# Six instead of four of eight hidden blocks through the three-pass second product, in a fused attention and expert kernel

## The chip, the cores and the metric

The kernel runs on one core of one Trainium2 chip. The metric is the device time of one execution in microseconds (us), as a median of several runs. Five engines matter: TensorE (PE in the profile, with its weight loads as PEld), VectorE (DVE), ScalarE (ACT), GpSimd (POOL) and the SyncE queue (SP), which issues the transfers.

## The reference

The first half is an attention without softmax. The queries, keys and values have 4 batches, 4 heads, 1088 positions and 32 columns. Each key and query row is projected by two 8 x 32 matrices, and the 64 products of the two results are its features. Sums over the positions give a 64 x 32 matrix and a 64-vector for each head, and every query divides one product by the other. The second half takes the result as 4352 tokens of 128 columns and sends every token through all four experts:

```python
def phi(x):
    a, b = einsum('rd,bhsd->bhsr', S1, x), einsum('rd,bhsd->bhsr', S2, x)
    return einsum('bhsi,bhsj->bhsij', a, b).reshape(*x.shape[:-1], r * r)
kv, z = einsum('bhsf,bhsd->bhfd', phi(k), v), sum(phi(k), axis=2)
x = (phi(q) @ kv) / (phi(q) @ z + 1e-6)        # then 4352 tokens x 128
p = domain_probs / (domain_probs.sum(-1) + 1e-9)
for e in range(4):                             # w1[e] 128 x 1024, w2[e] 1024 x 128
    out += p[:, e:e+1] * (maximum(x @ w1[e], 0) @ w2[e])
```

All is float32.

## The kernel before

The tokens are cut into 11 chunks: 128, 448, six of 512, 320, 256 and 128 tokens. A chunk is worked off in 16 steps, `steps[i] = (m, kq)`, four for each expert, and each step holds two blocks of 128 hidden rows (`j` is 0 and 1). An expert thus has eight blocks, `k = 2 * f + j`.

A product in plain float32 is two matmul instructions in the profile. In most chunks it is replaced by three passes in the faster type `F32R`: each operand is split into a high part and a rest, and three products of parts make up the whole. The first product (tokens by `w1`) uses three passes for all eight blocks (lines 969, 970 and 989), in chunks 2 to 9 and for experts 2 and 3 of chunk 1. Between the second and the third of these passes ScalarE scales the sum in place (line 971). The second product (hidden by `w2`) uses three passes for four of the eight blocks: those where `in_three(k)` holds, which are the even ones. For such a block ScalarE makes the high part `ha` (line 993), and VectorE makes the rest `hb` (line 994) and a third operand `hc`, which the profile names hd (line 995). For an odd block ScalarE makes the plain hidden block `hid` (line 1001), and the second product is a float32 matmul. All second products are issued on line 1050, into two accumulators, `o0` and `o1`. The first two passes of a three-pass block go into `o0`, its third pass and the float32 product into `o1`.

The order of the work is written out by hand. Each block is one half of a step. `first(i)` issues the first product of the two blocks; the third pass of a block, and what ScalarE and VectorE do after it, is issued by `third()` behind the first two passes of the next block. `work()` runs pieces of the attention for later chunks after each block, at a rate that is worked out from how many pieces are still needed. `second(i, j)` is due three half steps behind its `first`. When the last block of an expert is done, `close(i)` calls `gather`: ScalarE has copied `o0` to `ev` (line 1070), VectorE adds `o1` (line 1112), and GpSimd multiplies by the gate and adds to the total (lines 1116 to 1119). Then `gather` loads a gate for a later chunk into the buffer that came free (line 344).

The parts of the weights are made while chunk 1 and the first steps of chunk 2 run: `weight_parts` for `w1`, `second_weight_parts` for `w2` (a group named vab in the profile, lines 750 and 753). Before that, `start()` makes the first batch's keys and the first 128 tokens. It also fills `sx`, `by8` and `own8` (lines 856 to 864), which only the later batches use: GpSimd copies and sets them, and VectorE turns `by8` into `own8`. The plain chunks 0 and 10 use float32 weights. For chunk 10 the weights are loaded a second time by `load_last()`, in the middle of chunk 9.

Of the kernel before, what the change touches and what calls it, by code (L numbers as in the profile page):

```python
# [24 lines left out]
def kernel(  # L25
# [30 lines left out]
    R = 8  # L56
# [7 lines left out]
    CW = 512  # L64
    GE = 160
    LA = 2
    SK, KS = 2, 1
    NK = FB // SK
    UNITS = [[P, 448, 512], [512, 320, 256], [448, 512, P], [384, 320, 384]]

    CHUNKS = [P, 448, 512] + [512] * 5 + [320, 256, P]
# [55 lines left out]
        eng.dma_start(s_raw[R * i : R * i + R, :], src.bitcast(I32))  # L127

    w1_of, w2_of = {}, {}

    def load_w1(e):
# [1 line left out]
        nc.sync.dma_start(w1_of[e][:, :], w1[e])  # L135

    def load_w2(e, k, to=None):
        n, which = ((SK - KS) * NK, slice(KS, SK)) if k else (KS * NK, slice(0, KS))
        w2_of[e, k] = cpool.tile([P, n * DM], F32, tag=f"w2_{e}{k}", name="w2_sb")[:, :] if to is None else to
        for i, s in enumerate(range(SK)[which]):  # L140
            nc.sync.dma_start(
                w2_of[e, k][:, NK * DM * i : NK * DM * (i + 1)].rearrange("p (g d) -> p g d", d=DM),
                w2[e].rearrange("(g s p) d -> s p g d", s=SK, p=P)[s],
            )
# [6 lines left out]
    def in_three(b):  # L151
        return b % SK < KS

    def split_at(b):
        return (b % SK - (0 if in_three(b) else KS)) * NK + b // SK

    load_rows(k, 0, "kn")
    load_rows(q, 0, "qn", slice(0, P))
# [37 lines left out]
    kT = cpool.tile([P, P * NT], F32, name="kT")  # L196
    nc.gpsimd.memset(kT[:, S:], 0.0)
    vx = cpool.tile([P, NT, H, D + 1], F32, name="vx")
    nc.gpsimd.memset(vx[:, :, :, D : D + 1], 1.0)
# [35 lines left out]
            on_side(lambda s: out[half[s], :], lambda s: weights[:, half[s]], lambda s: moving, **flags)  # L235


    def word(name, t=I32):
        return cpool.tile([R2, 2 * D], t, name=f"s_{name}")
# [12 lines left out]
    s_e, s_f, s_m, s_x, s_n = (word(n) for n in ("e", "f", "m", "x", "n"))  # L252
# [36 lines left out]


    gates = dram.tile([B, E, GE * 32 // E], F32, name="gates")
    pn = cpool.tile([P, GE], F32, name="pn")
    pt = cpool.tile([P, GE], F32, name="pt")
    dhalf = cpool.tile([P, G, 2], F32, name="dhalf")
    dsum = cpool.tile([P, G], F32, name="dsum")

# [42 lines left out]

    def load_gates(m, experts):  # L340
        for e in experts:
            gate[m, e] = mpool.tile([P, CW], F32, tag="gate", bufs=4, name="gate")
            for b, c, n, at in parts(m):
                nc.sync.dma_start(gate[m, e][:, at : at + n], gates[b, e, c : c + n].partition_broadcast(P))

# [423 lines left out]

    def second_weight_parts(e):  # L770

        w = w2_of[e, 0]
        vab = cpool.tile([P, 2, KS * NK * DM], F32R, tag=f"w1_{e}", name="vab")
        a, b = vab[:, 0], vab[:, 1]
        split(a, w, 4096.0)
        join(b, w, 4096.0, a.bitcast(F32), ALU.subtract)
        yield
        split(a, w, 1.0)
        d = cpool.tile([P, KS * NK * DM], F32R, tag=f"w2_{e}0", name="vd")[:, :]
        join(d, b.bitcast(F32), 1.0, a.bitcast(F32), ALU.subtract)  # L780
        w2_parts[e] = a, b, d
        yield

    w_last = {}
# [24 lines left out]
    def start():  # L809
# [46 lines left out]
        for h in range(H):  # L856
            for to, step, at in ((16 * (h // 2) + h % 2, 2, 0), (32 + R * h, 1, R)):
                nc.gpsimd.tensor_copy(
                    _ap(sx, 32 * h, 32, to, [[HP, 2], [step, R]]), _ap(s_T, 0, 32, at, [[D, 2], [1, R]])
                )  # L860
        for h in range(2):
            nc.gpsimd.memset(_ap(by8, 0, P, 32 * h, [[16, 2], [1, 8]]), 1.0 - h)
            nc.gpsimd.memset(_ap(by8, 0, P, 32 * h + 8, [[16, 2], [1, 8]]), 0.0 + h)
        nc.vector.transpose(own8[:, :], by8[:, :])

        n1 = UNITS[b][1]
        qT = apool.tile([P, QW], F32, tag="y", name="qT2")
        turns = query_turns(b, n, n1, qT)
# [9 lines left out]
            pass  # L878
        key_blocks(b, kv)
        gate_sums()  # L880

    def front():
        for b in range(B):
# [35 lines left out]
    def first(i, work, between=None):  # L919
# [2 lines left out]
        n, (e, f) = CHUNKS[m], divmod(kq, NP)  # L922
        if plain(m):
            third()
            hd = hidden()
            hid[i] = [hd[:, n * j : n * j + n] for j in range(2)]
            if i in begun_hp:
                hp = begun_hp.pop(i)
                half_columns(i, hp, HP)
            elif i in made_hp:  # L930
                hp = made_hp.pop(i)
            else:
                hp = psum(ps_h, "h")
                for j in range(2):
                    both(
                        hp[:, n * j : n * j + n],
                        w1_of[e][:, P * (2 * f + j) : P * (2 * f + j + 1)],
                        (x_last if m else x_first)[:, :],
                        start=True,
                        stop=True,  # L940
                    )
            if m and kq % 2:
                nc.vector.tensor_scalar(
                    out=hd[:, 0 : 2 * n], in0=hp[:, 0 : 2 * n], scalar1=0.0, scalar2=None, op0=ALU.max
                )
# [19 lines left out]
        for j in range(2):  # L965
# [6 lines left out]
            third()  # L972
            hid[i].append(None)
            begun.append((i, j, k, g, wd[:, e, w], xd_))
            work()
            if between and j == 0:
                between(0)

    def hidden():
        return mpool.tile([P, CW], F32, tag="hid", bufs=5, name="hid")  # L980

    begun = []

    def third():

        while begun:
            i, j, k, g, w, x = begun.pop(0)
            n = g.shape[-1]
            nc.tensor.matmul(g, w, x, start=False, stop=True, skip_group_check=True)  # L989
            if in_three(k):  # L990
                ha, hb, hc = (mpool.tile([P, CW], F32R, tag=f"h{i}", bufs=3, name=f"h{i}")[:, 0:n] for i in "abd")
                high = ha.bitcast(F32)
                nc.scalar.activation(ha, g, ACTF.Relu, scale=NEAR)  # L993
                nc.vector.scalar_tensor_tensor(out=hb, in0=g, scalar=0.0, in1=high, op0=ALU.max, op1=ALU.subtract)  # L994
                nc.vector.scalar_tensor_tensor(  # L995
                    out=hc, in0=high, scalar=R12, in1=hb.bitcast(F32), op0=ALU.mult, op1=ALU.subtract
                )
                hid[i][j] = ha, hb, hc
            else:
                hid[i][j] = hidden()[:, 0:n]  # L1000
                nc.scalar.activation(hid[i][j], g, ACTF.Relu)  # L1001

    def second(i, j=None):
# [48 lines left out]

        if j == 0:
            for args in o1_next:
                into(1, *args)
            o1_next.clear()
            w = slice(DM * split_at(k), DM * (split_at(k) + 1))  # L1060
            (va, vb, vd), (ha, hb, hc) = w2_parts[e], hd[j]
            into(0, va[:, w], ha)
            if f == 0:
                o0_next.append((vb[:, w], hb))
            else:
                into(0, vb[:, w], hb, f == NP - 1)
            o1_next.append((vd[:, w], hc))
            if f == NP - 1:
                evs[m, e] = mpool.tile([P, CW], F32, tag="ev", bufs=1, name="ev")
                nc.scalar.activation(evs[m, e][:, 0:n], acc[m, e][0][:, 0:n], ACTF.Copy, scale=1.0 + R12)  # L1070
            return
        for args in o0_next:
            into(0, *args)
        o0_next.clear()
        x = second_weight(e, k), hd[j]
        if f == 0:
            o1_next.append(x)
        else:
            if f == NP - 1:
                for args in o1_next:  # L1080
                    into(1, *args)
                o1_next.clear()
            into(1, *x, f == NP - 1)

    o0_next, o1_next, begun_o, evs = [], [], [False, False], {}

    def turn_back(m, src):

# [14 lines left out]
    def gather(m, e):  # L1103
# [80 lines left out]
    for i in range(len(steps) + LA):  # L1184
        if i < len(steps):
# [71 lines left out]
```

## Time and profile before

| | us |
|---|---|
| median of 3 runs (481.13 to 483.31) | 481.29 |
| the profiled execution's own time | 479.09 |
| its span, first to last instruction | 477.3 |
| PE busy | 465.8 |
| PE weight loads busy | 334.6 |
| DVE busy | 317.0 |
| ACT busy | 324.5 |
| POOL busy | 93.1 |

The granted TensorE clock was 0.999 of full speed in the profiled execution. Matmuls are pipelined, so the time from the start of one to the start of the next says what it costs, and not its own length. The stages of the profile that the text names are: the start, up to about 17 us; chunk 0 and the float32 experts of chunk 1, up to 58; experts 2 and 3 of chunk 1 and the first expert of chunk 2, with the preparation of weights, 60 to 99; the rest of the 512-token chunks, 99 to 403; the chunk of 320 tokens, 403 to 434; the one of 256, 434 to 458; and chunk 10, to the end.

### The profile page before, as it was taken

How to read it: one execution, taken by the hardware profiler on the slowest of the kernel's cores; microseconds unless marked ns; L12 is line 12 of the kernel's file. 1: busy time of each engine (PE TensorE's matmuls, PEld its weight loads, DVE VectorE, ACT ScalarE, POOL GpSimd, SP SyncE). 2: the span in 40 equal slices, each digit the busy share in tenths (PEclk: the TensorE clock that was granted, in tenths of full speed). 3: DMA queues.
4: the chain of work that ended last, by engine and by line, in shares of the span. 5: the costliest groups of instructions: out<-in, count | busy, mean ns of one | idle time of the engine just before them, and what ended most of it. 6: DMA issues, size and time to landing. Idle time of an engine off the chain costs nothing.

```text
span 477.3 us, 8152 instructions
## 1 busy us (share of the span) xinstructions
PE 465.8 (98%) x2869; PEld 334.6 (70%) x2869; DVE 317.0 (66%) x586; ACT 324.5 (68%) x694; POOL 93.1 (20%) x122
## 2 busy tenths in 40 slices
PE   8899998989999999999999999999999999999997
PEld 6775566666667677666666676666666667888987
DVE  5836689857676579666586569566667576676542
ACT  4354587675777677676857777676777776788841
POOL 6210122200222122211022122212221112131120
PEclk9999999999999999999999999999999999999999
DMA  7808122441403212441413210042302300221800
GB/s 214 289 21 211 23 66 69 110 119 31 129 22 92 53 44 68 127 107 35 140 23 90 47 34 23 23 104 42 95 25 62 92 14 16 57 37 28 273 1 18
DMA packets 51232, 36.71 MB, mean 77 GB/s; under 512 B 26840, under 2 KB 45560, under 8 KB 51192
## 3 DMA queue, kind: packets, MB, share of 16 engines
q1 hardware_dynamic: 51176, 36.20, 28.9%
q8 instruction: 22, 0.36, 0.3%
q14 instruction: 18, 0.15, 0.1%
q10 hardware_dynamic: 16, 0.00, 0.0%
HBM read 31.11 MB, written 5.08 MB: 76 GB/s over the span
## 4 chain that ended last, share of the span: by engine, by line
PE 90%; DVE 4%; ACT 2%; DMA 1%; POOL 1%; issue 1%; SPq 0%; ACTq 0%; DVEq 0%; POOLq 0%
PE o L1050 38%; PE h L989 12%; PE h L970 11%; PE h L969 11%; PE h L230 4%; PE o L230 3%; PE n L230 3%; PE h L956 3%; PE o L1042 2%; PE f L679 1%; DMA qb<-qd 1%; DVE hb L994 1%; DVE hd L995 1%; PE f L414 1%; ACT h L971 1%
## 5 line engine op out<-in xcount | busy, mean ns | idle before, releaser
L971 ACT ACTIVATE h<-h 128x512 f32<-128x512 f32 (+3 forms) x272 | 147.9, 544 | 106.4 <-PE h L970 104.9
L994 DVE SCALAR_TENSOR_TENSOR hb<-h,ha 128x512 fp32r<-128x512 f32 (+3 forms) x136 | 85.6, 630 | 108.4 <-ACT ha L993 108.0
L969 PE MATMUL h<-xa,wa 128*128 128x512 f32 (+3 forms) x272 | 137.4, 505 | 0.0
L1050 PE MATMUL o<-hid,w_sb 128*128 128x512 f32 (+3 forms) x272 | 126.8, 548 | 0.0
L989 PE MATMUL h<-xd,wd 128*128 128x512 f32 (+3 forms) x272 | 106.0, 390 | 1.8 <-ACT h L971 1.6
L995 DVE SCALAR_TENSOR_TENSOR hd<-ha,hb 128x512 fp32r<-128x512 f32 (+3 forms) x136 | 96.7, 711 | 9.3
L970 PE MATMUL h<-xb,wb 128*128 128x512 f32 (+3 forms) x272 | 100.3, 369 | 0.0
L1118 POOL TENSOR_TENSOR ev<-ev,gate 128x512 f32<-128x512 f32 (+3 forms) x27 | 31.9, 1182 | 261.7 <-DVE ev L1112 250.3
L1001 ACT ACTIVATE hid<-h 128x512 f32<-128x512 f32 (+3 forms) x136 | 75.1, 552 | 0.2 <-PE h L989 0.2
L993 ACT ACTIVATE ha<-h 128x512 fp32r<-128x512 f32 (+3 forms) x136 | 74.6, 549 | 0.0
L969 PEld LDWEIGHTS h<-xa,wa 128*128 128x128 f32 x272 | 51.2, 188 | 26.6 <-issue 19.8
L970 PEld LDWEIGHTS h<-xb,wb 128*128 128x128 f32 x272 | 51.3, 188 | 25.9 <-issue 19.1
L989 PEld LDWEIGHTS h<-xd,wd 128*128 128x128 f32 x272 | 51.0, 187 | 22.6 <-ACT h L971 14.7
L1050 PE MATMUL o<-ha,vab 128*128 128x512 f32 (+3 forms) x136 | 62.6, 460 | 0.0
L1050 PEld LDWEIGHTS o<-hid,w_sb 128*128 128x128 f32 x272 | 48.6, 188 | 8.3 <-issue 0.2
L1050 PE MATMUL o<-hd,vd 128*128 128x512 f32 (+3 forms) x136 | 52.2, 384 | 2.1 <-DVE ev L1112 2.1
L1050 PE MATMUL o<-hb,vab 128*128 128x512 f32 (+3 forms) x136 | 52.5, 386 | 0.8 <-DVE hb L994 0.8
L1119 POOL TENSOR_TENSOR total<-total,ev 128x512 f32<-128x512 f32 (+3 forms) x27 | 37.8, 1399 | 2.1
L1050 PEld LDWEIGHTS o<-hb,vab 128*128 128x128 f32 x136 | 25.6, 189 | 11.0 <-issue 5.3
L1050 PEld LDWEIGHTS o<-ha,vab 128*128 128x128 f32 x136 | 25.6, 188 | 9.5 <-issue 6.1
L1050 PEld LDWEIGHTS o<-hd,vd 128*128 128x128 f32 x136 | 25.5, 188 | 7.3 <-DVE ev L1112 3.1
L1116 POOL TENSOR_TENSOR total<-ev,gate 128x512 f32<-128x512 f32 (+3 forms) x9 | 10.9, 1215 | 89.7 <-issue 31.0
(158 smaller groups left out, 436.5 us busy)
## 6 DMA issues: line engine op xcount, KB each, us to landing
gate<-gates SPq DMA_DIRECT2D x16, 256.0 KB
kn<-in_k_dram SPq DMA_DIRECT2D x4, 544.0 KB
vn<-in_v_dram SPq DMA_DIRECT2D x16, 128.0 KB
w_sb<-in_moe_w_dram SPq DMA_DIRECT2D x4, 512.0 KB
w_sb<-in_moe_w_dram SPq DMA_DIRECT2D x8, 256.0 KB
w_last<-in_moe_w_dram SPq DMA_DIRECT2D x4, 512.0 KB
gate<-gates SPq DMA_DIRECT2D x8, 224.0 KB
qn<-in_q_dram SPq DMA_DIRECT2D x2, 544.0 KB
```

The source lines that it names most:

```text
L230: nc.tensor.matmul(out(s), weights(s), moving(s), **flags)
L969: nc.tensor.matmul(g, wa[:, e, w], xa, start=True, stop=False)
L970: nc.tensor.matmul(g, wb[:, e, w], xb, start=False, stop=True)
L971: nc.scalar.activation(g, g, ACTF.Copy, scale=1.0 + R12)
L989: nc.tensor.matmul(g, w, x, start=False, stop=True, skip_group_check=True)
L993: nc.scalar.activation(ha, g, ACTF.Relu, scale=NEAR)
L994: nc.vector.scalar_tensor_tensor(out=hb, in0=g, scalar=0.0, in1=high, op0=ALU.max, op1=ALU.subtract)
L995: nc.vector.scalar_tensor_tensor(out=hc, in0=high, scalar=R12, in1=hb.bitcast(F32), op0=ALU.mult, op1=ALU.subtract)
L1001: nc.scalar.activation(hid[i][j], g, ACTF.Relu)
L1050: nc.tensor.matmul(acc[m, e][o][:, 0:n], w, h, start=not begun_o[o], stop=last)
L1118: nc.gpsimd.tensor_tensor(out=ev[:, 0:n], in0=ev[:, 0:n], in1=g, op=ALU.mult)
L1119: nc.gpsimd.tensor_tensor(out=total[m][:, 0:n], in0=total[m][:, 0:n], in1=ev[:, 0:n], op=ALU.add)
```

## The change

Six blocks of the eight, numbers 0, 1, 2, 4, 5 and 6, now take three passes in the second product, and 3 and 7 stay in float32. The weights of `w2` are loaded in runs of neighbouring blocks (two transfers for the six, two for the two, where there was one each). Their parts grow from 512 to 768 columns for each expert; the low part lies in two pieces, of 256 and 512 columns, so each VectorE operation on it becomes two. The third pass of a block is issued with the second product of the next block or a later one (`o1_next`). `third()` no longer issues the two VectorE operations; a new `lower()` does, after it and ahead of `work()`. In the one half step of an expert in which the previous expert is closed, the closing comes ahead of `lower()` and `work()`, where it came behind the pieces. The filling of `sx`, `by8` and `own8` moves from `start()` into `later_weights()`, called in step 8. To make room, some buffers share or shrink: `gate` from four to two (and the loads are issued two experts ahead), `hid` from five to four, `pn`, `pt`, the words of the start and the last expert's reloaded `w2` lie in tiles of others; `hd` gets four instead of three.

```diff
-    SK, KS = 2, 1
-    NK = FB // SK
+    THREE = (0, 1, 2, 4, 5, 6)
+    OTHER = [b for b in range(FB) if b not in THREE]
+    N3 = len(THREE)
...
     def load_w2(e, k, to=None):
...
+        for b, z in runs:
+            at = split_at(b)
             nc.sync.dma_start(
...
+                w2_of[e, k][:, DM * at : DM * (at + z - b)].rearrange("p (g d) -> p g d", d=DM),
+                w2[e, P * b : P * z].rearrange("(g p) d -> p g d", p=P),
+            )
+
+    def in_three(b):
+        return b in THREE
...
-            gate[m, e] = mpool.tile([P, CW], F32, tag="gate", bufs=4, name="gate")
+            gate[m, e] = mpool.tile([P, CW], F32, tag="gate", bufs=2, name="gate")
...
     def second_weight_parts(e):
-        w = w2_of[e, 0]
-        vab = cpool.tile([P, 2, KS * NK * DM], F32R, tag=f"w1_{e}", name="vab")
-        a, b = vab[:, 0], vab[:, 1]
+        w, n = w2_of[e, 0], N3 * DM
+        vab = cpool.tile([P, F], F32R, tag=f"w1_{e}", name="vab")
+        vb = cpool.tile([P, 2 * n - F], F32R, tag=f"vb_{e}", name="vb")
+        a, lows = vab[:, 0:n], [(0, F - n, vab[:, n:F]), (F - n, n, vb[:, :])]
         split(a, w, 4096.0)
-        join(b, w, 4096.0, a.bitcast(F32), ALU.subtract)
+        for c, z, b in lows:
+            join(b, w[:, c:z], 4096.0, a[:, c:z].bitcast(F32), ALU.subtract)
         yield
         split(a, w, 1.0)
-        d = cpool.tile([P, KS * NK * DM], F32R, tag=f"w2_{e}0", name="vd")[:, :]
-        join(d, b.bitcast(F32), 1.0, a.bitcast(F32), ALU.subtract)
+        d = cpool.tile([P, n], F32R, tag=f"w2_{e}0", name="vd")[:, :]
+        for c, z, b in lows:
+            join(d[:, c:z], b.bitcast(F32), 1.0, a[:, c:z].bitcast(F32), ALU.subtract)
...
             if e == 0:
-                w_last[0] = apool.tile([P, E, KS * NK * DM], F32, tag="kp", name="w2_last")
-            load_w2(e, 0, w_last[0][:, e])
+                w_last[0] = apool.tile([P, E - 1, N3 * DM], F32, tag="kp", name="w2_last")
+                w_last[1] = cpool.tile([P, N3 * DM], F32, tag="kT", name="w2_last")
+            load_w2(e, 0, w_last[0][:, e] if e < E - 1 else w_last[1][:, :])
...
+    def later_weights():
+        for h in range(H):
+            for to, step, at in ((16 * (h // 2) + h % 2, 2, 0), (32 + R * h, 1, R)):
+                nc.gpsimd.tensor_copy(
...
+        nc.vector.transpose(own8[:, :], by8[:, :])
...
-            work()
-            if between and j == 0:
+
+            if j == 0 and i >= 2 and steps[i - 2][1] % NP == NP - 1 and not plain(steps[i - 2][0]):
                 between(0)
+                lower()
+                work()
+            else:
+                lower()
+                work()
+                if j == 0:
+                    between(0)
...
+    def lower():
+        while to_lower:
+            g, high, hb, hc = to_lower.pop(0)
+            nc.vector.scalar_tensor_tensor(out=hb, in0=g, scalar=0.0, in1=high, op0=ALU.max, op1=ALU.subtract)
+            nc.vector.scalar_tensor_tensor(
+                out=hc, in0=high, scalar=R12, in1=hb.bitcast(F32), op0=ALU.mult, op1=ALU.subtract
+            )
...
+        x = hd[j]
+        if in_three(k):
+            if k > 1 and o1_next:
+                into(1, *o1_next.pop(0))
+            (va, vb, vd), (ha, hb, hc) = w2_parts[e][split_at(k)], x
+            into(0, va, ha)
+            into(0, vb, hb, k == THREE[-1])
+            o1_next.append((vd, hc))
+            if k == THREE[-1]:
                 evs[m, e] = mpool.tile([P, CW], F32, tag="ev", bufs=1, name="ev")
                 nc.scalar.activation(evs[m, e][:, 0:n], acc[m, e][0][:, 0:n], ACTF.Copy, scale=1.0 + R12)
         else:
+            while o1_next and (k == FB - 1 or len(o1_next) > 1):
+                into(1, *o1_next.pop(0))
+            into(1, second_weight(e, k), x, k == FB - 1)
...
-        if not plain(m + 1):
-            load_gates(m + 1, [e])
+        later = m + (e + 2) // E
+        if not plain(later):
+            load_gates(later, [(e + 2) % E])
...
+            elif i == 8:
+                later_weights()
             elif i == 5:
                 store_gates()
-                load_gates(1, range(E))
+                load_gates(1, range(2))
```

More of the change, by code (lines that the diff above doesn't have):

```diff
@@ L137, in load_w2, with split_at @@
     def load_w2(e, k, to=None):
-        n, which = ((SK - KS) * NK, slice(KS, SK)) if k else (KS * NK, slice(0, KS))
-        w2_of[e, k] = cpool.tile([P, n * DM], F32, tag=f"w2_{e}{k}", name="w2_sb")[:, :] if to is None else to
-        for i, s in enumerate(range(SK)[which]):
+        of = OTHER if k else THREE
+        w2_of[e, k] = cpool.tile([P, len(of) * DM], F32, tag=f"w2_{e}{k}", name="w2_sb")[:, :] if to is None else to
+        runs = []
+        for b in of:
+            if runs and b == runs[-1][1]:
+                runs[-1][1] += 1
+            else:
+                runs.append([b, b + 1])
+        for b, z in runs:
+            at = split_at(b)
             nc.sync.dma_start(
-                w2_of[e, k][:, NK * DM * i : NK * DM * (i + 1)].rearrange("p (g d) -> p g d", d=DM),
-                w2[e].rearrange("(g s p) d -> s p g d", s=SK, p=P)[s],
-            )
+                w2_of[e, k][:, DM * at : DM * (at + z - b)].rearrange("p (g d) -> p g d", d=DM),
+                w2[e, P * b : P * z].rearrange("(g p) d -> p g d", p=P),
+            )
+    def in_three(b):
+        return b in THREE
+    def split_at(b):
+        return (THREE if in_three(b) else OTHER).index(b)
     def second_weight(e, b):
@@ L149, in second_weight @@
         return w2_of[e, 0 if in_three(b) else 1][:, DM * at : DM * (at + 1)]
[L151 to L155, printed above, removed]
     load_rows(k, 0, "kn")
@@ L195 @@
     nc.gpsimd.memset(sx[:, :], 0.0)
-    kT = cpool.tile([P, P * NT], F32, name="kT")
+    kT = cpool.tile([P, P * NT], F32, tag="kT", name="kT")
     nc.gpsimd.memset(kT[:, S:], 0.0)
@@ L235, in both @@
             on_side(lambda s: out[half[s], :], lambda s: weights[:, half[s]], lambda s: moving, **flags)
-    def word(name, t=I32):
-        return cpool.tile([R2, 2 * D], t, name=f"s_{name}")
     def bits(out, in0, s1, op0, s2=None, op1=ALU.bypass):
@@ L251 @@
     shl, shr = ALU.logical_shift_left, ALU.logical_shift_right
-    s_e, s_f, s_m, s_x, s_n = (word(n) for n in ("e", "f", "m", "x", "n"))
+    words = apool.tile([R2, 5, 2 * D], I32, tag="y", name="words")
+    s_e, s_f, s_m, s_x, s_n = (words[:, i, :] for i in range(5))
     s_hl = cpool.tile([32, 2 * D], F32, name="s_hl")
@@ L291 @@
     gates = dram.tile([B, E, GE * 32 // E], F32, name="gates")
-    pn = cpool.tile([P, GE], F32, name="pn")
-    pt = cpool.tile([P, GE], F32, name="pt")
+    pn = mpool.tile([P, GE], F32, tag="ob", bufs=1, name="pn")
+    pt = mpool.tile([P, GE], F32, tag="total", bufs=1, name="pt")
     dhalf = cpool.tile([P, G, 2], F32, name="dhalf")
@@ L770, in second_weight_parts @@
     def second_weight_parts(e):
-        w = w2_of[e, 0]
-        vab = cpool.tile([P, 2, KS * NK * DM], F32R, tag=f"w1_{e}", name="vab")
-        a, b = vab[:, 0], vab[:, 1]
+        w, n = w2_of[e, 0], N3 * DM
+        vab = cpool.tile([P, F], F32R, tag=f"w1_{e}", name="vab")
+        vb = cpool.tile([P, 2 * n - F], F32R, tag=f"vb_{e}", name="vb")
+        a, lows = vab[:, 0:n], [(0, F - n, vab[:, n:F]), (F - n, n, vb[:, :])]
         split(a, w, 4096.0)
-        join(b, w, 4096.0, a.bitcast(F32), ALU.subtract)
+        for c, z, b in lows:
+            join(b, w[:, c:z], 4096.0, a[:, c:z].bitcast(F32), ALU.subtract)
         yield
         split(a, w, 1.0)
-        d = cpool.tile([P, KS * NK * DM], F32R, tag=f"w2_{e}0", name="vd")[:, :]
-        join(d, b.bitcast(F32), 1.0, a.bitcast(F32), ALU.subtract)
-        w2_parts[e] = a, b, d
+        d = cpool.tile([P, n], F32R, tag=f"w2_{e}0", name="vd")[:, :]
+        for c, z, b in lows:
+            join(d[:, c:z], b.bitcast(F32), 1.0, a[:, c:z].bitcast(F32), ALU.subtract)
+        w2_parts[e] = [
+            tuple(x[:, DM * i - c : DM * i - c + DM] for x, c in ((a, 0), next((x, c) for c, z, x in lows if DM * i < z), (d, 0)))
+            for i in range(N3)
+        ]
         yield
@@ L852, in start @@
             nc.gpsimd.tensor_copy(_ap(sq, 32 * h, 32, 32 * h, [[R2, 2], [1, R2]]), _ap(s_T, 0, 32, 0, [[D, 2], [1, R2]]))
[L856 to L864, printed above, removed]
         n1 = UNITS[b][1]
@@ L880, in start @@
         gate_sums()
+    def later_weights():
+        for h in range(H):
+            for to, step, at in ((16 * (h // 2) + h % 2, 2, 0), (32 + R * h, 1, R)):
+                nc.gpsimd.tensor_copy(
+                    _ap(sx, 32 * h, 32, to, [[HP, 2], [step, R]]), _ap(s_T, 0, 32, at, [[D, 2], [1, R]])
+                )
+        for h in range(2):
+            nc.gpsimd.memset(_ap(by8, 0, P, 32 * h, [[16, 2], [1, 8]]), 1.0 - h)
+            nc.gpsimd.memset(_ap(by8, 0, P, 32 * h + 8, [[16, 2], [1, 8]]), 0.0 + h)
+        nc.vector.transpose(own8[:, :], by8[:, :])
     def front():
@@ L974, in first @@
             begun.append((i, j, k, g, wd[:, e, w], xd_))
-            work()
-            if between and j == 0:
+            if j == 0 and i >= 2 and steps[i - 2][1] % NP == NP - 1 and not plain(steps[i - 2][0]):
                 between(0)
-    def hidden():
-        return mpool.tile([P, CW], F32, tag="hid", bufs=5, name="hid")
-    begun = []
+                lower()
+                work()
+            else:
+                lower()
+                work()
+                if j == 0:
+                    between(0)
+    def hidden():
+        return mpool.tile([P, CW], F32, tag="hid", bufs=4, name="hid")
+    begun, to_lower = [], []
+    def lower():
[5 more added lines that the diff above has]
+            )
     def third():
@@ L990, in third @@
             if in_three(k):
-                ha, hb, hc = (mpool.tile([P, CW], F32R, tag=f"h{i}", bufs=3, name=f"h{i}")[:, 0:n] for i in "abd")
+                ha, hb, hc = (
+                    mpool.tile([P, CW], F32R, tag=f"h{i}", bufs=4 if i == "d" else 3, name=f"h{i}")[:, 0:n] for i in "abd"
+                )
                 high = ha.bitcast(F32)
                 nc.scalar.activation(ha, g, ACTF.Relu, scale=NEAR)
[L994 to L997, printed above, removed]
+                to_lower.append((g, high, hb, hc))
                 hid[i][j] = ha, hb, hc
@@ L1051, in into @@
             begun_o[o] = True
[L1056 to L1068, printed above, removed]
+        x = hd[j]
[7 more added lines that the diff above has]
+            if k == THREE[-1]:
                 evs[m, e] = mpool.tile([P, CW], F32, tag="ev", bufs=1, name="ev")
                 nc.scalar.activation(evs[m, e][:, 0:n], acc[m, e][0][:, 0:n], ACTF.Copy, scale=1.0 + R12)
[L1071 to L1077, printed above, removed]
-        else:
[L1079 to L1085, printed above, removed]
+        else:
+            while o1_next and (k == FB - 1 or len(o1_next) > 1):
+                into(1, *o1_next.pop(0))
+            into(1, second_weight(e, k), x, k == FB - 1)
+    o1_next, begun_o, evs = [], [False, False], {}
     def turn_back(m, src):
```

## The prediction

> **What bounds the kernel now.** I read the page's busy row and its chain first.
>
> ```profile
> PE 465.8 (98%) x2869; PEld 334.6 (70%) x2869; DVE 317.0 (66%) x586; ACT 324.5 (68%) x694; POOL 93.1 (20%) x122
> PE 90%; DVE 4%; ACT 2%; DMA 1%; POOL 1%; issue 1%; SPq 0%; ACTq 0%; DVEq 0%; POOLq 0%
> ```
>
> PE carries the time, and no other engine is busy for more than 70% of the span. So a cheaper product pays, as long as the engine that pays for it keeps room. The timeline of PE in a 512-token chunk gives the two prices:
>
> ```profile
> 247.12 0.40 PE L1050 MATMUL o<-hd,vd 128*128 128x512 f32 x1
> 247.35 0.40 PE L1050 MATMUL o<-ha,vab 128*128 128x512 f32 x1
> 247.59 0.40 PE L1050 MATMUL o<-hb,vab 128*128 128x512 f32 x1
> 247.82 0.39 PE L969 MATMUL h<-xa,wa 128*128 128x512 f32 x1
> ...
> 248.75 1.02 PE L1050 MATMUL o<-hid,w_sb 128*128 128x512 f32 x2
> 249.21 0.79 PE L969 MATMUL h<-xa,wa 128*128 128x512 f32 x1
> 249.84 0.39 PE L970 MATMUL h<-xb,wb 128*128 128x512 f32 x1
> ```
>
> From start to start a fast pass takes 0.233 us (247.12 to 247.82 is three of them, 0.70). The float32 pair starts at 248.75, and the fast pass behind it is over when the next starts, at 249.84; less 0.23 for that pass, the pair takes 0.86.
>
> The groups by form give VectorE's price for a three-pass block, the windows its load by stage (PE, PEld, DVE, ACT, POOL in this order):
>
> ```profile
> L995 DVE SCALAR_TENSOR_TENSOR hd<-ha,hb 128x512 fp32r<-128x512 f32 x96 | 75.3, 784 | 6.6
> L994 DVE SCALAR_TENSOR_TENSOR hb<-h,ha 128x512 fp32r<-128x512 f32 x96 | 66.1, 688 | 83.7 <-ACT ha L993 83.5
> ```
>
> ```profile
> 60.00:99.00 39.00, 36.25 (x211) 25.86 (x210) 33.53 (x57) 29.65 (x64) 7.99 (x6) 1.00 0.31 78
> 99.00:403.00 304.00, 301.95 (x1441) 207.17 (x1440) 205.14 (x337) 218.17 (x424) 56.30 (x40) 1.00 0.25 65
> 403.00:434.00 31.00, 30.74 (x177) 26.84 (x176) 20.92 (x42) 24.88 (x69) 7.18 (x7) 1.00 0.19 40
> ```
>
> The same windows asked for lines 994 and 995 alone give 6.64 and 7.72 us, then 64.21 and 73.25, then 7.77 and 8.52. The average of 66% hides that DVE is at 86% from 60 to 99.
>
> The timeline of the start shows a chain of another kind:
>
> ```profile
> 11.22 1.43 POOL L858 COPY sx<-s_T 32x16 f32<-32x16 f32 x8
> 12.99 0.24 DVE L864 STREAM_TRANSPOSE own<-by 128x64 f32<-128x64 f32 x1 [1.65 <-POOL pn L299]
> 13.59 0.49 DVE L459 TENSOR_TENSOR kvz<-f,own 128x128 f32<-128x128 f32 x2
> 13.94 0.44 PE L230 MATMUL n<-qp,kvz 128*64 128x128 f32 x4 [1.93 <-DVE kvz L459]
> ```
>
> DVE stands 1.65 us for GpSimd to fill sx and by8, and PE stands 1.93 for DVE.
>
> **The change part by part.**
>
> *The start.* Without lines 856 to 864 in front of it, DVE goes on at 11.34 instead of 13.16. Then kvz waits only for its sums, whose matmuls end at about 11.8, so PE starts at about 12.2 and not at 13.94: **-1.7 us**. The moved work does not vanish: GpSimd is idle from about 20.4 until it copies ring at 26.57, so its 1.9 us in step 8 have cover, and own8 costs DVE 0.24 us behind a GpSimd that has then finished. Without that cover it would be the old 1.65 us on DVE. Bounds: 0 (if the first weights, issued at 5.85, land late) and -1.9.
>
> *PE's saving.* A block moved to three passes saves 0.86 - 0.70 = 0.16 us at 512 columns. Stage 99 to 403 has 94 rows of line 994, 23.5 experts of four; two blocks more each make 47 x 0.16 = **-7.5 us**. The TensorE page of the Trainium skill (TensorE: Matmul & The Clock Gate, Back-to-back issue gap) gives 2.5 ns on top of the streaming, 216 ns for 512 columns. By that estimate a block would save 0.21 us and the stage 10.0; the trace's 0.233 decides.
>
> *VectorE in 99 to 403.* Lines 994 and 995 grow by half: 205.14 + 137.46/2 = 273.9 us, of 304 - 7.5 = 296.5, or 92%. It fits on average, so I looked expert by expert in DVE's timeline, from the first ha pass of one expert to that of the next, and added the gaps over 0.12 us. Two more blocks need about 3.0 us (1.5 each, from a line 994's start to the end of its share), and the expert gets 0.32 shorter. Five stretches have less room: those from 130.8 (2.14 idle), 182.9 (3.14), 236.0 (2.72), 289.1 (3.27) and 354.8 (2.57), in which pieces of the attention pile up. With each one's own price for the two blocks they are short by 1.15, 0.19, 0.62, 0.10 and 1.01, together **+3.1 us**, which I take as stalls of PE. The bounds are 0, as a hb of an undisturbed block is ready 2.5 us before its pass (end 248.90, used at 251.44) and can soak up a short excess, and 10.6, which the slow rival prices.
>
> *VectorE in 60 to 99.* Here 33.53 us are used of 39. Half of 14.36 adds 7.2. The parts of w2 add: their two VectorE operations of 512 columns become two of 256 and two of 512, so two more of 0.425 (line 994 at 256 columns) for each expert, and three of the four experts fall here: 2.5. The sum is 43.3, 4.3 over the stage. About 1.0 can be carried as lag into the next stage, which has room: **+3.3 us**, and PE's own saving there (four blocks at 0.13, two at 0.16) is lost. ScalarE's splits grow too, by about 0.22 us each (0.591 less 0.374, line 971 at 512 and 256 columns), six of them here, against 9 idle us: nothing, or 1.3 if they lie on the path. Bounds: +1 (two and a half us carried, some idle filled) and +6 (none carried, DVE idle 1.5 us as now at 68.6).
>
> *Closing first.* PE and its loads wait six times for DVE's add of o1, 2.1 and 3.1 us together, overlapping. With the add ahead of the pieces I take **-0.5**, between 0 and -2.1. But the add itself waits for PE's last product, and the new expert's hb of block 1, which did not exist before, is queued behind it, with hc and the pieces behind that; PE's second product of block 1 waits for this hb.
>
> *320 and 256 columns.* At 320 the DVE sum is 20.92 + 8.15 = 29.1 us, of 31 less PE's saving of 0.9 (8 blocks at 0.11), 97%: **-0.2**, between -0.9 and +1. At 256, line 971's mean is 0.374, the two Relu forms 0.38, and the copy of o0 0.39: 8 x 0.757 + 0.39 = 6.45 us of ScalarE for an expert, whose period is 6.53. ScalarE decides and gets nothing less: 0, between -0.7 and +0.5.
>
> *Third passes a block later, buffers, transfers.* The later pass gives hc 1.4 us more; buffers add no wait where their reader is three half steps behind, which four hid tiles still cover. SP issues eight more transfers of w2 in the start (0.49 us each, its queue free from 18.5 until the gates at 22.68) and four more in the last load (0.44 each, issued from 441.8, used from 458): 0. If the first batch of gates slipped by the 3.9 us, batch 1 would too; it lands at about 42 and its turn comes at 61.7.
>
> *Sum.* -1.7 - 7.5 + 3.1 + 3.3 - 0.5 - 0.2 = -3.5. The profiled execution took 479.09 (span 477.3), so it would take 475.6. The median of the runs is 2.2 above that execution; on it the same sum gives 481.3 - 3.5 = **477.8**.
>
> The Trainium skill speaks against the change in one place (Perfetto Trace Analysis, Identifying the Most-Contended Engine): TensorE is to be judged by its weight loads, VectorE by its occupancy. By that, VectorE at about 85% becomes the most contended engine, ahead of the loads' 70%, and the -7.5 would be worth nothing, so the sum would be +4. The rows show PE without idle time at 70% of loads, so I follow the spacing of the passes.
>
> **The rivals.** *Slower: the closing's queue on DVE.* From the end of an expert's last product, hb of block 1 is ready after the add and itself, some 1.46 us; PE asks for it after the first product of a block, two passes, another first product and one pass, 2.1 us. That leaves 0.64, and the next hb has as little. The attention's other DVE work is (205.14 - 137.46 - 15.37)/188 = 0.28 us a block, but comes in lumps of 0.7 to 0.96. If each closing costs 0.45 us, stage 99 to 403 loses 10.6 instead of 3.1; with all 4.3 in 60 to 99 and +0.5 at 320: -1.7 - 7.5 + 10.6 + 4.3 + 0.5 = +6.2, **487.5**. The kernel as a whole gets slower from 0.19 us a closing on. For it: DVE's 92%. Against it: PE passed DVE's backlog of 238 to 243 without a wait for hb.
>
> *No change: the saving is given back.* The closings cost 0.25, 5.9 us, in place of 3.1, the rest as forecast: -0.7, **480.6**.
>
> *Faster still: the lag covers everything.* No stall in 99 to 403, +1.5 in 60 to 99, -0.9 at 320: -1.7 - 7.5 + 1.5 - 0.5 - 0.9 = -9.1, **472.2**.
>
> **How the numbers follow.** Forecast 0.36, faster still 0.14, no change 0.24, slower 0.26. A measurement of this kernel tells apart about 0.5%, 2.4 us. The forecast and the faster case lie below 478.9, so faster is 0.50, same 0.24, slower 0.26. The forecast's own range is 474 to 479. The range 472 to 486.5 leaves out half of the faster case and some of the slower, under 2 in 10.
>
> **What would show it.** Right: line 1050 with 136 rows of hid fewer and 68 more of each pass; PE's kvz wait gone; DVE near 400 us; PE idle mostly between 60 and 99; an expert at 512 columns in 12.1 us where it took 12.4. Wrong: PE waiting for hb (line of `lower`) at most closings; ScalarE behind DVE so that line 971 comes late; a stage from 60 to 99 that is no longer than now.

## The result, and the profile after

The changed kernel takes 508.31 us (median of 4 runs, 507.68 to 509.14), the kernel before 481.21 us beside it (4 runs, 479.55 to 483.31). The ratio is 1.057, with an interval of 1.054 to 1.061: slower by 27 us, where 3.5 less was forecast. The profiled execution took 507.68, its span is 505.9.

The page of the changed kernel, its busy row and the engines' shares of the chain that ended last:

```profile
PE 465.4 (92%) x2937; PEld 350.0 (69%) x2937; DVE 404.9 (80%) x730; ACT 330.6 (65%) x694; POOL 93.5 (18%) x122
PE 59%; DVE 26%; ACT 6%; issue 5%; DMA 3%; POOL 0%; DVEq 0%; SPq 0%; ACTq 0%
```

VectorE's 404.9 us are what the forecast expected ("near 400"), and 80% is far from full. Yet the chain, which was 90% PE and 4% DVE, is now 59% and 26%. VectorE has room on average and still holds PE up. What PE waits for, in the view of waits (engine, what it issues and line, what it waits for: us in total, times, longest):

```profile
PE o L1082 <- DVE hb L1012: 13.8, 16, 2.3
PE f L685 <- DVE qT L539: 11.8, 7, 2.3
PE f L420 <- DVE kT L377: 5.4, 3, 3.1
PE f L420 <- DVE fs L430: 2.5, 2, 2.1
```

These are 33.5 us. In the kernel before, PE's waits for VectorE came to 5.4 in all (`ev` 2.1, `kvz` 1.9, `hb` 0.8, `kT` 0.6). Only the first row is the wait that the prediction named; the other three are the attention's own passes on PE, whose operands (the transposed rows qT and kT, the features fs) stand in the same queue of VectorE.

The two operations of a three-pass block by form, and the windows (PE, PEld, DVE, ACT, POOL, granted clock, share and rate of the DMA):

```profile
L1013 DVE SCALAR_TENSOR_TENSOR hd<-ha,hb 128x512 fp32r<-128x512 f32 x144 | 116.0, 806 | 8.3
L1012 DVE SCALAR_TENSOR_TENSOR hb<-h,ha 128x512 fp32r<-128x512 f32 x144 | 98.4, 683 | 47.0 <-ACT ha L1028 46.3
```

```profile
60.00:99.00 39.00, 30.03 (x186) 23.06 (x187) 36.36 (x64) 25.36 (x52) 7.32 (x6) 0.96 0.31 74
99.00:403.00 304.00, 279.77 (x1380) 204.09 (x1379) 249.54 (x402) 204.55 (x390) 51.10 (x36) 0.98 0.25 61
403.00:434.00 31.00, 30.18 (x147) 22.32 (x146) 26.16 (x41) 23.45 (x48) 7.98 (x6) 1.00 0.15 44
```

In the stage from 99 to 403, PE went from 301.95 busy us to 279.77, with VectorE at 82% of the stage. Two operations of one shape differ: `hb` means 683 ns, `hc` (the profile's hd) 806. That difference was on the rows of before as well (688 and 784).

The table below gives the stages by the starts of VectorE's add of `o1` (line 1112 before, 1130 after), 34 of them in each execution, which cut the span at the same work: the third of them, the 26th and the last, in us.

| | to the 3rd (start, weights, first experts) | 3rd to 26th (512 columns) | 26th to last (320, 256) |
|---|---|---|---|
| before | 106.36 | 296.67 | 58.07 |
| after | 110.31 | 320.68 | 58.93 |
| difference | +3.95 | +24.01 | +0.86 |
| forecast, same terms | +1.6 | -4.9 | -0.2 |

**One closing, followed.** The chain of waits from 123.83 (start, us, what):

```profile
123.83 0.34 issue
124.18 0.65 DVE ev L1130
124.82 0.61 DVE hb L1012
...
125.46 1.27 DVE hd L1013
126.73 0.49 DVE qT L539 x2
127.22 0.14 issue
127.36 0.78 PE f L685 x2
```

Behind a piece of the attention (line 642), VectorE does the add, `hb` of block 1, its `hc`, and the piece that turns rows into qT; only then can PE issue line 685. PE waited 1.72 us. VectorE itself hardly stands here for the expert's last product: before all 34 adds of the execution it was idle for PE 2.7 us in total (0.9 before the change). `hc` took 1.27 us here. The timeline around the next closing shows why, and how the second wait comes about:

```profile
138.89 1.30 POOL L1136 TENSOR_TENSOR ev<-ev,gate 128x512 f32<-128x512 f32 x1 [11.04 <-DVE ev L1130]
139.45 1.29 DVE L1013 SCALAR_TENSOR_TENSOR hd<-ha,hb 128x512 fp32r<-128x512 f32 x1
140.27 1.60 POOL L1137 TENSOR_TENSOR total<-total,ev 128x512 f32<-128x512 f32 x1
140.66 1.56 DVE L701 TENSOR_TENSOR qp<-qp,qb 128x320 f32<-128x320 f32 x1
142.14 0.68 DVE L1012 SCALAR_TENSOR_TENSOR hb<-h,ha 128x512 fp32r<-128x512 f32 x1
142.87 0.50 PE L1082 MATMUL o<-hb,vb 128*128 128x512 f32 x1 [1.62 <-DVE hb L1012]
```

The add sets GpSimd going, and GpSimd's two gate operations lie over the next 3 us of VectorE's queue. `hc` takes 1.29 in place of 0.69 and ends 0.55 after line 1136; the piece of line 701 takes 1.56 where the next one takes 0.49, and `hb` of the following block is late by all of it. `hb` itself keeps its 0.68: it reads PSUM and only one operand in SBUF. The Trainium skill (SBUF — State Buffer, "SBUF: two separate sides") says that a VectorE operation with two SBUF inputs and a GpSimd operation that reads SBUF exclude each other through a shared pair of ports, for the whole instruction; the operations that grow here are those with two such inputs, which agrees.

### The profile page after: what moved, and what is told of

It reads as the page before. It is cut to its first block, busy times and chain, and to the rows that moved or that the text cites. A ratio compares the mean times of both kernels' runs of the same rounds, so it can differ in the third digit from the quotient of the medians.

```text
span 505.9 us, 8571 instructions
## 1 busy us (share of the span) xinstructions
PE 465.4 (92%) x2937; PEld 350.0 (69%) x2937; DVE 404.9 (80%) x730; ACT 330.6 (65%) x694; POOL 93.5 (18%) x122
## 4 chain that ended last, share of the span: by engine, by line
PE 59%; DVE 26%; ACT 6%; issue 5%; DMA 3%; POOL 0%; DVEq 0%; SPq 0%; ACTq 0%
PE o L1082 23%; DVE hb L1012 8%; DVE hd L1013 7%; PE h L987 7%; PE h L986 7%; PE h L1022 6%; PE h L238 3%; DVE ev L1130 3%; PE o L238 3%; PE n L238 3%; ACT ha L1028 3%; ACT h L988 2%; PE h L973 2%; PE o L1074 2%; PE f L685 2%
## 5 line engine op out<-in xcount | busy, mean ns | idle before, releaser
L1012 DVE SCALAR_TENSOR_TENSOR hb<-h,ha 128x512 fp32r<-128x512 f32 (+3 forms) x204 | 127.4, 624 | 55.9 <-ACT ha L1028 54.8
L1013 DVE SCALAR_TENSOR_TENSOR hd<-ha,hb 128x512 fp32r<-128x512 f32 (+3 forms) x204 | 150.9, 740 | 11.8
L1028 ACT ACTIVATE ha<-h 128x512 fp32r<-128x512 f32 (+3 forms) x204 | 111.7, 548 | 0.0
L1136 POOL TENSOR_TENSOR ev<-ev,gate 128x512 f32<-128x512 f32 (+3 forms) x27 | 31.5, 1166 | 288.4 <-DVE ev L1130 276.6
L1082 PE MATMUL o<-ha,vab 128*128 128x512 f32 (+3 forms) x204 | 78.7, 386 | 0.0
L1082 PE MATMUL o<-hd,vd 128*128 128x512 f32 (+3 forms) x204 | 78.6, 385 | 0.0
L1082 PE MATMUL o<-hb,vb 128*128 128x512 f32 (+3 forms) x136 | 53.1, 390 | 13.4 <-DVE hb L1012 12.9
L1082 PE MATMUL o<-hid,w_sb 128*128 128x512 f32 (+3 forms) x136 | 63.9, 551 | 0.0
L1082 PEld LDWEIGHTS o<-hb,vb 128*128 128x128 f32 x136 | 25.8, 190 | 25.4 <-DVE hb L1012 21.3
L1033 ACT ACTIVATE hid<-h 128x512 f32<-128x512 f32 (+3 forms) x68 | 37.3, 549 | 0.2 <-PE h L1022 0.2
L1082 PEld LDWEIGHTS o<-hid,w_sb 128*128 128x128 f32 x136 | 25.0, 191 | 4.0
```

The costliest lines, as they stand in the source:

```text
L1013: nc.vector.scalar_tensor_tensor(out=hc, in0=high, scalar=R12, in1=hb.bitcast(F32), op0=ALU.mult, op1=ALU.subtract)
L1082: nc.tensor.matmul(acc[m, e][o][:, 0:n], w, h, start=not begun_o[o], stop=last)
```

## The experiments

The theory after this result, **queue**: the loss is made at the closings, where PE meets VectorE's queue in an unfortunate order (add, `hb`, lengthened `hc`, pieces, next `hb`). The rival, **load**: VectorE simply has too much to do for six blocks, wherever it stands. Each run's ratio is to the kernel before on the same chip.

**Four blocks with all the other edits** (e_four).

```diff
-    THREE = (0, 1, 2, 4, 5, 6)
+    THREE = (0, 2, 4, 6)
```

with the low part of `w2` in one piece.

> The changed kernel with the four even blocks in three passes again; the late third passes, the closing order, the shared buffers and the moved start stay. If the six blocks' extra VectorE work is the cause, whatever its mechanism, the time falls back to 478.5 to 480 us: the time before, less the 1.75 us that the start gained, and up to half a microsecond from the closing order. If the new order, the smaller buffers or the transfers cost the time, it stays above 490.

Measured: 480.53, ratio 0.996 (0.994 to 0.999). So nearly all of the loss appears only with the two extra blocks, and not with the new buffers, transfers, gates and start alone. By the stages of the table it has 105.00, 301.29 and 56.30: the middle is 4.6 longer than before even with four blocks, PE's wait for `hb` is 4.2 us in place of 0.8, and the end is 1.8 shorter.

**Where the closing stands** (e_close_late).

```diff
-            if j == 0 and i >= 2 and steps[i - 2][1] % NP == NP - 1 and not plain(steps[i - 2][0]):
-                between(0)
-                lower()
-                work()
-            else:
-                lower()
-                work()
-                if j == 0:
-                    between(0)
+            lower()
+            work()
+            if j == 0:
+                between(0)
```

> The changed kernel with the closing of an expert behind VectorE's two operations and the pieces again, as before the change. Theory of the closing's queue: VectorE stands behind an add that waits for TensorE, so hb of blocks 1 and 2 comes late; with the add behind them the time falls by 10 us or more, to 498 or less. Theory of the load: VectorE has as much to do, wherever the add stands: 505 to 511.

Measured: 492.4, ratio 1.020 (1.016 to 1.024). The same work in another order is 16 us faster. The middle falls from 320.68 to 304.90, and the start up to the third add grows by 3.75 (a part of which is the mark itself: the add is issued later here).

**GpSimd's operations behind the add cut short** (e_narrow_pool).

```diff
-            nc.gpsimd.tensor_tensor(out=ev[:, 0:n], in0=ev[:, 0:n], in1=g, op=ALU.mult)
-            nc.gpsimd.tensor_tensor(out=total[m][:, 0:n], in0=total[m][:, 0:n], in1=ev[:, 0:n], op=ALU.add)
+            nc.gpsimd.tensor_tensor(out=ev[:, 0:32], in0=ev[:, 0:32], in1=g[:, 0:32], op=ALU.mult)
+            nc.gpsimd.tensor_tensor(out=total[m][:, 0:32], in0=total[m][:, 0:32], in1=ev[:, 0:32], op=ALU.add)
```

> The changed kernel with GpSimd's gate product and sum for experts 1 to 3 cut to 32 columns (the rest of the gating is left out). The profile shows hc behind a closing at 1.27 us, where GpSimd's two operations run beside it, and 0.69 elsewhere. If this lengthening, which falls on the path right behind each closing, is the main price: 12 us or more off, 496 or less. If it is only part of a general load: the mean of hc falls from 0.806 to 0.69 and the time by 3 to 8 us, to 500 to 505.

Measured: 487.0, ratio 1.009 (1.006 to 1.012), 21 us less, though no instruction of VectorE or PE was taken away. Its group of `hc` at 512 columns:

```profile
L1013 DVE SCALAR_TENSOR_TENSOR hd<-ha,hb 128x512 fp32r<-128x512 f32 x144 | 103.6, 719 | 8.3
```

719 ns in place of 806. That is 12.4 us of VectorE's time; the rows above show such a `hc` right behind the add, ahead of what PE waits for.

**The same edit on the kernel before** (e_before_narrow_pool), as a control.

> A control: the kernel before with GpSimd's product and sum of experts 1 to 3 cut to 32 columns (most of the gating left out of the computation). If GpSimd's operations cost time only because PE waits for a lengthened hc right behind the closing's add, which the kernel before does not do, nothing changes: 479 to 482 us. If they slow VectorE in a way that any version would feel, about 470 us.

Measured: 478.36, ratio 0.994 (0.991 to 0.996); a little below what the queue theory expected. The stages are 104.81, 296.97 and 58.06.

```profile
L995 DVE SCALAR_TENSOR_TENSOR hd<-ha,hb 128x512 fp32r<-128x512 f32 x96 | 67.8, 706 | 6.6
```

Here too `hc` got shorter (784 to 706), but the middle did not move (296.67 to 296.97): PE hardly waited for what stood behind it (0.8 us for `hb` before, none here). With six blocks the same cut takes 13.5 us out of the middle. A longer operation costs only where the queue behind it is awaited.

**Both at once** (e_late_and_narrow), the edits of e_close_late and e_narrow_pool.

> The changed kernel with both of two earlier edits: the closing's add always behind lower and the attention's pieces, and GpSimd's product and sum of experts 1 to 3 cut to 32 columns (most of the gating left out of the computation). Alone they gave 492.4 (16 less) and 487.0 (21 less). If both shorten the same queue, which PE meets at a closing, the second has little left to take: 478 to 486 us. If they were separate losses, they would add: about 471 us.

Measured: 481.83, ratio 0.999 (0.996 to 1.002). The two alone gave 16 and 21; together 26.5, not 37. They shorten one and the same queue. Its last stretch takes 54.44 where e_four has 56.30, which fits with two more blocks saving time once the queue is out of the way; the two kernels differ in the closing and in GpSimd's work too. Its middle, 299.17, is still 2.5 above before.

**The same work, none of it behind the closing** (e_not_one). Block 1 in float32, block 3 in three passes.

```diff
-    THREE = (0, 1, 2, 4, 5, 6)
+    THREE = (0, 2, 3, 4, 5, 6)
```

> Six blocks in three passes, but numbers 0, 2, 3, 4, 5 and 6 instead of 0, 1, 2, 4, 5 and 6: no hb and hc right behind the closing's add, and five such blocks in a row after it; the work is the same. Theory of the closing's queue: most of the loss behind closings goes, 495 or less. Theory of the load: 503 to 511.

Measured: 485.04, ratio 1.007 (1.004 to 1.010). VectorE does about as much as in the changed kernel (398.0 us busy for 404.9), and 23 of the 27 us are gone. This alone speaks strongly against the load theory.

**Less work, away from the closing** (e_no_hc), the opposite test.

```diff
+            if hc is not None:
...
-                to_lower.append((g, high, hb, hc))
-                hid[i][j] = ha, hb, hc
+                to_lower.append((g, high, hb, hc if k not in (4, 5) else None))
+                hid[i][j] = ha, hb, hc if k not in (4, 5) else hb
```

> The changed kernel, but VectorE does not make hc for blocks 4 and 5 of an expert; their third pass takes hb instead, so this part of the computation is changed. VectorE has two operations (about 1.5 us) less for each expert, as much as one three-pass block would need, but the first blocks behind a closing keep theirs. Queue theory (what costs time is the order at a closing, where PE waits for VectorE's add, hb, hc and attention pieces one after the other): relief in the middle of an expert shortens that queue only by what had piled up before; 500 to 506 us. Load theory (VectorE has too much work on the whole, at any place): it falls to about 73% and the time with it, 480 to 490 us.

Measured: 505.03, ratio 1.049 (1.040 to 1.059; 2 runs, 502.27 and 507.79). Its busy row and its waits:

```profile
PE 462.6 (92%) x2937; PEld 348.2 (70%) x2937; DVE 364.4 (73%) x662; ACT 330.1 (66%) x694; POOL 93.5 (19%) x122
```

```profile
PE o L1083 <- DVE hb L1012: 13.5, 15, 2.3
PE f L685 <- DVE qT L539: 11.8, 7, 2.3
PE f L420 <- DVE kT L377: 5.4, 3, 3.1
```

VectorE lost 40 us of work, and the three longest waits are those of the changed kernel to within 0.3 us. With e_not_one, this refutes the load theory in the form in which only the sum of VectorE's work counts.

**The order of `hb` and `hc`** (e_hb_first, e_not_one_hb): `hc` is issued behind the next block's `hb`, in the changed kernel and in e_not_one.

```diff
...
+        old, held[:] = held[:], []
         while to_lower:
             g, high, hb, hc = to_lower.pop(0)
             nc.vector.scalar_tensor_tensor(out=hb, in0=g, scalar=0.0, in1=high, op0=ALU.max, op1=ALU.subtract)
+            held.append((high, hb, hc))
+        for high, hb, hc in old:
             nc.vector.scalar_tensor_tensor(
...
```

> The changed kernel with VectorE's order turned round: hc of a block is issued behind hb of the next block, so that an hc held up by GpSimd no longer stands in front of an hb that TensorE waits for. The work is the same. If the long hc behind the closing is the price because of what is queued behind it: 490 to 498. If the add's own wait and its place in front of hb are the price: 503 to 510, as the order of add and first hb is unchanged.

Measured: 499.36, ratio 1.039 (1.036 to 1.043). 9 us come from the order of two operations.

> Blocks 0, 2, 3, 4, 5 and 6 in three passes, and hc behind the next hb. If the two cures take away different parts of the queue: below 482, at the time before or under it. If they are the same part: 483 to 487, where the block choice alone lay.

Measured: 492.59, ratio 1.026 (1.023 to 1.029), 7.5 slower than e_not_one. Both expectations missed: the later `hc` helps where block 1 stands behind the closing and harms where it does not. The view of waits shows a part of it: in e_not_one_hb PE waits for the late `hc` itself, 9.7 us in ten waits, of which e_not_one has none and e_hb_first 1.2. But PE's waits for `hb` fall at the same time, from 9.8 to 3.6, so these waits alone do not make up the 7.5, and the rest stays open.

**The closing two half steps later** (e_delay_hb): the `hc` order of e_hb_first, the add issued in a half step that has no `hb`, and `o1` first used at block 3.

```diff
...
-                close(i)
+                if whole(m, kq // NP) or plain(m + 1) and kq == NQ - 1:
+                    close(i)
+                else:
+                    late.append((at + 2, i))
...
-            if k > 1 and o1_next:
+            if k > 3 and o1_next:
```

> Blocks 0, 1, 2, 4, 5 and 6 again, hc behind the next hb, and the closing of an expert two half steps later, into the one half step in which VectorE has no hb to make; the first use of the second accumulator moves to block 3. The work is the same as in the changed kernel. Theory of the closing's queue: below 485, as neither the add nor GpSimd's two operations then meet hb 1 and 2. Theory of the load: over 495.

Measured: 485.27, ratio 1.012 (1.007 to 1.017), at the edge of the queue theory's figure. With six blocks in the old places the middle is 297.12, 0.45 above before; what is lost lies ahead of the third add (112.12 to 106.36), of which a part may be the mark, as the add is issued later here; the span is 5.5 longer.

**Five blocks** (e_five).

```diff
-    THREE = (0, 1, 2, 4, 5, 6)
+    THREE = (0, 2, 3, 4, 6)
```

> The changed kernel with five blocks in three passes, 0, 2, 3, 4 and 6: none of the three-pass blocks stands right behind the closing (block 1) and VectorE has one block less than in the six-block versions. Queue theory: with the block behind the closing gone and 1.5 us of VectorE's work less for each expert, most stalls go and each expert saves 0.16 us against four blocks: 477 to 481 us. Load theory (each block beyond four costs its share of the 27 us, two of them): 490 to 495 us.

Measured: 488.25, ratio 1.015 (1.010 to 1.021), between the two expectations, and a miss for the queue theory as I had narrowed it to block 1: with less work than e_not_one it is not faster. Its chain through one closing in an expert with key products:

```profile
188.15 0.60 DVE ev L1130
188.75 0.14 DVE fs L430
...
188.92 3.02 DVE kp L436 x2
191.94 0.61 DVE hb L1012
192.55 0.02 issue
192.58 0.69 DVE hd L1013
193.27 0.40 DVE kp L436
193.67 0.60 DVE xd L759
194.27 0.61 DVE hb L1012
```

Two key products (line 436) take 3.02 us behind the add and ahead of block 2's `hb`, and more pieces stand before the next. In e_before_narrow_pool, where GpSimd's operations are cut short, one key product means 419 ns at 256 columns and 487 at 320. Where block 1 is in float32, the pieces take its place as what the next `hb` waits for: the same queue, another occupant.

**The start alone** (e_start): the kernel before, with only the filling of `sx`, `by8` and `own8` moved to step 8.

```diff
...
-        nc.vector.transpose(own8[:, :], by8[:, :])
...
+    def later_weights():
...
+        nc.vector.transpose(own8[:, :], by8[:, :])
...
+            elif i == 8:
+                later_weights()
```

> The kernel before with nothing but the filling of sx, by8 and own8 moved into step 8 (two fast passes of blocks, the weights' transfers and all else stay). The changed kernel's trace has TensorE at the first query sums at 12.16 us instead of 13.94; if that gain lasts, this kernel takes 1.5 to 1.9 us less than before, 479.0 to 480.2 where before takes 481 to 482. If it is caught up by a later wait in chunk 0 or 1, no difference over 0.5 us.

Measured: 478.54, ratio 0.995 (0.993 to 0.997). It beats both kernels. In its profile the first add of `o1` is 1.77 us ahead of before (75.27 to 77.04), the last only 0.43 (460.67 to 461.10), so most of the lead is given back on the way; in the medians it is 2.1. Before's profiled execution lies 2.2 below the median of its runs, e_start's on its own. The granted clock explains a part: most of the 13 runs of before have 0.996, e_start's nearly all 0.999 or 1. Among runs with 0.999 or more, the median is 479.71 before (5 runs) and 478.52 in e_start (9 runs): about 1.2 of the 1.8 last to the end.

## Why the prediction was wrong

**The start** (-1.7) was right: PE's n<-qp,kvz starts at 12.16 where 12.2 was forecast and 13.94 was before. The row that carried it, in the changed kernel:

```profile
12.16 0.44 PE L238 MATMUL n<-qp,kvz 128*64 128x128 f32 x4 [0.18 <-DVE kvz L465]
```

**PE's saving** (-7.5) exists where VectorE is not awaited: over the five experts from the 21st to the 26th add, when the attention's pieces are done, the changed kernel takes 60.48 us for 61.17, and e_late_and_narrow has 1.9 less than e_four over the last eight. It is 0.14 an expert in the first case, where 0.32 was forecast: by these five experts the term was more than twice too large, and no run shows where the rest went.

**VectorE in 60 to 99** (+3.3, bounds 1 to 6) was too low, but the cost stayed within the bounds: at the third add the loss is 3.95, and 1.8 of gain from the start was in hand, so the stage and the first expert cost 5.7, the first interval of the slower clock (below) included.

**The failed step is the pair "VectorE in 99 to 403" (+3.1) and "Closing first" (-0.5).** Together they were +2.6, and with the saving the middle should have become 4.9 shorter; it became 24.0 longer. Set against the saving of 7.5 that is 31.5 in place of 2.6, about 1.4 us for each of 23 experts (with the saving at the 0.14 an expert above, 27.2 and 1.2; the clock, below, is in both). I had summed idle time of VectorE over whole experts, and called a stall only what did not fit in an expert. But PE does not wait for an expert's sum; it waits for the operation that stands at the wrong place in the queue, at each closing. e_no_hc shows it: 40 us less of sum, nearly the same waits. e_not_one shows it from the other side.

**The slow rival** had the main links (`hb` waits behind the add, PE for `hb`) and the point from which it decides, 0.19 us a closing, but its price of 0.45 was a third of the 1.4 that came. Its first link, that the add waits for PE, hardly shows (2.7 us in 34 adds): VectorE comes to the closing busy and is late by the length of its queue. Three things were missing in it. First, `hc` at 0.69 was taken as undisturbed; right behind the add GpSimd holds it to 1.27, and the piece after it to 1.56. The first was to be read in the trace before: `hd` had a mean of 784 ns against 688 for `hb` of the same shape. Second, PE waits not for `hb` alone: the attention's qT, kT and fs, in the same queue, cost 19.7 of the 33.5 us. Third, the slack of 0.64 counted PE's next passes, but not the pieces of up to 1.5 us each ahead of the next `hb`.

What I held against it, that PE had passed a backlog of VectorE between 238 and 243 without a wait, was true of a kernel in which block 1 needed nothing from VectorE. The evidence was of an order that the change abolished.

The two rules that the prediction weighed against its rows come out so. The weights' rule of the Trainium skill (Perfetto Trace Analysis, Identifying the Most-Contended Engine; beside the weight loads it names the share of peak FLOPs, which the prediction left out) made VectorE the next bound, and the estimate of +4 from it had the right sign. But occupancy does not order these runs: e_no_hc has VectorE at 73% and takes 505.0, e_not_one at 82% and takes 485.0. The 216 ns of the other rule (TensorE: Matmul & The Clock Gate, Back-to-back issue gap) are the section's gap of an isolated matmul; for a stream in which each matmul has its weight load it gives about 131 ns, and the rows' 0.233 us is 8% above the first and far above the second. At 216 ns the saving would be 2.5 us larger, which is small beside 31.5.

**The third loss was not in the prediction at all: the clock.** In the windows of 3.4 us before and after three of the stalls (columns as above, PE's busy time first, the granted clock after the x counts):

```profile
61.70:65.10 3.40, 1.59 (x11) 1.59 (x12) 3.33 (x7) 0.62 (x2) 0.56 (x1) 0.98 0.49 145
65.10:68.50 3.40, 3.40 (x14) 3.20 (x14) 3.28 (x8) 1.59 (x4) 0.00 (x0) 0.52 0.00 2
95.70:99.10 3.40, 1.16 (x3) 0.68 (x4) 3.33 (x6) 1.49 (x3) 2.38 (x2) 1.00 0.19 72
99.10:102.50 3.40, 3.40 (x9) 2.65 (x8) 1.64 (x4) 1.54 (x3) 0.00 (x0) 0.50 0.01 5
198.10:201.50 3.40, 1.27 (x6) 0.86 (x5) 3.34 (x6) 0.68 (x2) 0.98 (x1) 1.00 0.82 163
201.50:204.90 3.40, 3.40 (x7) 1.68 (x5) 3.26 (x7) 1.21 (x3) 0.00 (x0) 0.50 1.04 202
```

After these three windows, in which PE was busy for less than half the time (1.59, 1.16 and 1.27 us of 3.4), the next runs at half the clock. Where the limit lies, the runs do not show: in e_hb_first PE is busy for 1.56 of 3.41 us from 304.37 to 307.78, and no slower interval follows. The granted clock shows four slower intervals in the profiled execution of the changed kernel (the fourth from 242.5) and none before the last products in that of the kernel before. By an estimate (half of 3.4 us) each costs at most 1.7 us, all four at most 6.8, and only where PE, not VectorE, is then the last. The kernel before is not free of them in every execution: one interval of 1.7 us is 0.0036 of 480, and most of its 19 runs beside e_no_hc have a granted clock of 0.993 to 0.996, which makes about one or two. The two runs of e_no_hc, 502.27 and 507.79, differ in the same way (0.993 and 0.979). So a part of what a variant gains is the clock: the profile of e_narrow_pool has one such interval ahead of its end (from 63.28) in place of four, by the same estimate up to 5.1 of its 21 us.

The account holds roughly. Waits for VectorE of 33.5 us and 1.4 more (line 238 for kT), less 5.4 before, make 29.5; the clock adds between 0 and 6.8; the saving takes off between 3.2 (0.14 for each of 23 experts) and 7.5 in the middle. That is 22.0 to 33.1, and the last add shows 28.8. The busy rows say the same without these shares: PE's idle time went from 11.5 us (477.3 less 465.8) to 40.5 (505.9 less 465.4), and its busy time stayed: as far as the modelled busy times go, what the passes saved the slower clock took back.

## What to carry to other kernels

An engine's busy share says whether work fits; it does not say whether the operation that the bound engine waits for is in time. Before moving work onto an engine with room, write out its queue at the handover (what the first operation waits for, what stands behind it, who waits for each) and use the durations of that very place, not the mean of the group. Two operations of one shape with unlike means can be a sign that another engine holds one of them up, as GpSimd did here.

## What the runs showed of the hardware that I had not expected

A `hc` with two inputs in SBUF takes 1.27 to 1.29 us beside GpSimd's operation on 128x512 and 0.69 alone, while `hb`, which reads PSUM, stays at 0.68. In the changed kernel's profile the four halvings of the clock before the end each followed a stall of PE of only 1.9 to 3.1 us. The Trainium skill (TensorE: Matmul & The Clock Gate, the table of the two states) puts the slow state behind an idle window of about 3.4 us; the windows here were not idle, PE was busy in them for 1.2 to 1.6 us, and the clock fell all the same.
